# A channel-mix weight split on one Trainium2 core: the sign carried by the slope of a leaky rectifier instead of a join of sign and low bits on VectorE

## Chip, cores and metric

The kernel runs on one core of a Trainium2 chip. The metric is the device time of one execution in microseconds (us); smaller is better. A core has a matrix engine (TensorE, PE in the profile), VectorE (DVE), ScalarE (ACT), GpSimd (POOL) and SyncE (SP), which issues all of this kernel's data transfers. Each engine runs its own instructions strictly in the order in which they were written.

## What is computed

```python
def reference(q, k, v, mem_k, mem_v, moe_mu_k, moe_mu_r, moe_w_k, moe_w_v, moe_w_r):
    # chunked local attention: B=4, H=8, S=768, D=64; 32 queries see 16 + 32 + 8 keys and 8 memory keys
    for c in range(24):
        scores = 0.125 * q_c @ k_full.T
        a = softmax(scores)
        out[:, :, c_start:c_end] = a @ v_full
    x = out.transpose(0, 2, 1, 3).reshape(4, 768, 512)
    # channel mix
    x_prev = x shifted by one token
    xk = mu_k * x + (1.0 - mu_k) * x_prev
    xr = mu_r * x + (1.0 - mu_r) * x_prev
    k = np.maximum(xk @ w_k, 0.0)          # w_k: 512 x 1024
    v = k * k @ w_v                        # w_v: 1024 x 512
    return sigmoid(xr @ w_r) * v           # w_r: 512 x 512
```

The three weight matrices are float64 in memory: they are a normal draw divided by a numpy square root. The other inputs are float32.

## The kernel before

**The products.** The channel mix is done in pairs of float32r numbers: each float32 operand is split into a high part (a cast to float32r) and a low part (the operand minus its high part), and each product is three matmuls, high by high, high by low and low by high.

**The weights.** A weight is loaded as 64-bit words, 1 MB (128 x 1024 words) at a time, in ten chunks: two of `w_r` (raw0, raw1), four of `w_k` (raw2 to raw5), four of `w_v` (raw6 to raw9). For each chunk `weight(i)` makes float32 out of float64 by handling bits:
- `f_abs` (ACT): the upper 32-bit word of each float64, read as a float32, has the sign, 8 of the 11 exponent bits as its exponent, and 3 exponent bits and 20 fraction bits as its fraction. Its absolute value times 2^-112 (`TINY`) moves the exponent so that it fits after a shift. The result goes to `mag`.
- `f_low` (DVE): two instructions, in place in the lower words: the lower word shifted right by 29 (its 3 top bits stay), and then the sign bit of the upper word joined to them.
- `f_join` (DVE): `mag` shifted left by 3, joined with what `f_low` left. That is the float32 weight.
- `f_hi` (ACT or DVE) casts it to float32r, `f_lo` (DVE or POOL) subtracts. The results are `wrh`/`wrl`, `wkh`/`wkl`, `wvh`/`wvl`, which stay in place for the whole kernel.

**The attention** is done in 24 tiles of 128 queries: load `qk` and `vw`, scores `s` (PE), maximum and difference (DVE), exponent (ACT), sum and reciprocal (DVE), the scaling of `e` (DVE or POOL), transposes into `pt` (PE), two copies into `aTz` (ACT or DVE), the product `px` (PE), a copy into `xT` (ACT or DVE).

**The channel mix** is done in 12 units of 256 tokens (two attention tiles): `prep` makes `df`, `xf` and their splits `xh`, `xl` on DVE, ACT and POOL; then PE runs the gate product `pr` (48 matmuls), the first layer `ph` (four blocks of 24 matmuls), and the second layer `pv` (48 matmuls, each of its two token groups in two halves). Between the layers ACT does the rectifier, the square and the cast `kh`, and DVE or POOL `kl`.

**The order.** Nothing is left to a scheduler at run time. A planner in the kernel (`Plan`) holds a list of steps, each with the engine or engines that may do it, a cost in us by the planner's own reckoning, the steps that it needs, and the buffers that it takes. It places the steps one by one on the engine that would finish each first, and the instructions are then written in the order of the planned starts. A changed cost thus moves steps in the order, and from one engine to another. On PE the order of the products is given by a written list (`te_order`). Before the first `ph` block, where the plan leaves PE without work, the loop at the end of the kernel writes fill matmuls on a tile of zeros (`warm`, line 590), one for each 0.22 us of the planned gap. PE runs these in line with its other instructions.

**Buffers.** The loads of `raw` and `qk` share three buffers (`big`): a load waits until the last reader of the load three places earlier has finished. For a weight chunk that last reader is `f_join`. A load of `qk4` waits in this way for the join of raw3, one of raw5 for the join of raw2. `mag`, `df` and `xf` share five (`x4`).

Of the kernel before, what the change touches and what calls it, by code (L numbers as in the profile page):

```python
# [8 lines left out]
F32 = mybir.dt.float32  # L9
F32R = mybir.dt.float32r  # L10
I64 = mybir.dt.int64
U32 = mybir.dt.uint32
AF = mybir.ActivationFunctionType
ALU = mybir.AluOpType
# [14 lines left out]
TINY = 2.0**-112  # L29
# [34 lines left out]
class Plan:  # L64
# [7 lines left out]
    def op(self, alts, fn, deps=(), new=(), use=(), due=1e9):  # L72
        if isinstance(alts, tuple):
            alts = [alts]
        o = Op([(a + (False,))[:3] for a in alts], fn, deps, new, use, due)
        o.seq = len(self.ops)
        self.ops.append(o)
        return o
# [80 lines left out]
def local_attention__then__channel_mix(  # L159
# [11 lines left out]
    nc = tc.nc  # L171
# [10 lines left out]
    def sb(tag, shape, name, dt=F32):  # L182
        return work.tile(shape, dt, tag=tag, name=name, bufs=bufs.get(tag, 1))
# [26 lines left out]
    op = plan.op  # L210
    T = {}

    def copy(e, dst, src):
        if e is nc.scalar:
            e.copy(dst, src)  # L215
        else:
            e.tensor_copy(dst, src)  # L217

    def either(**alts):
        return [(n, *alts[n]) for n in alts]  # L220
# [13 lines left out]
    def weight(i):  # L234
        src, (hi, lo), k = chunks[i]
        h, l = hi[k], lo[k]

        def f_load():
            T["raw", i] = sb("big", [P, 2 * DM], f"raw{i}", I64)
            if src is w_k:  # L240
                nc.sync.dma_start(T["raw", i], src[k * P : (k + 1) * P])
            else:
                nc.sync.dma_start(
                    T["raw", i].rearrange("p (t n) -> p t n", t=2),
                    src[2 * k * P : 2 * (k + 1) * P].rearrange("(t p) n -> p t n", p=P),
                )

        def word(j, dt):
            return T["raw", i].bitcast(dt).rearrange("p (n t) -> p n t", t=2)[:, :, j]

        def f_abs():
            m = T["mag", i] = sb("x4", [P, 2 * DM], f"mag{i}")
            nc.scalar.activation(m, word(1, F32), AF.Abs, scale=TINY)

        def f_low():
            nc.vector.tensor_scalar(word(0, U32), word(0, U32), 29, None, ALU.logical_shift_right)  # L258
            nc.vector.scalar_tensor_tensor(  # L259
                word(0, U32), word(1, U32), 0x80000000, word(0, U32), ALU.bitwise_and, ALU.bitwise_or  # L260
            )

        def f_join():
            mi = T["mag", i].bitcast(U32)
            nc.vector.scalar_tensor_tensor(mi, mi, 3, word(0, U32), ALU.logical_shift_left, ALU.bitwise_or)  # L265

        def f_hi(e):
            copy(e, h, T["mag", i])

        def f_lo(e):  # L270
            e.tensor_sub(l, T["mag", i], h.bitcast(F32))  # L271

        raw, mag = Slot("big"), Slot("x4")
        a = op(("dma", 3.0), f_load, new=[raw])
        b = op(("act", 0.95), f_abs, [a], new=[mag], use=[raw])
        g = op(("dve", 1.75, True), f_low, [a], use=[raw])
        j = op(("dve", 1.15, True), f_join, [b, g], use=[raw, mag])
        hh = op(either(act=(0.95,), dve=(0.62, True)), f_hi, [j], use=[mag])
        ll = op(either(dve=(1.15, True), pool=(2.5, True)), f_lo, [hh], use=[mag])
        wdone[id(hi), k] = (hh, ll)  # L280
# [292 lines left out]
    for i in range(len(chunks)):  # L573
        weight(i)
# [69 lines left out]
```

## Time and profile before

| | us |
|---|---|
| median of 3 runs (lowest to highest) | 447.37 (446.78 to 447.56) |
| the profiled execution, its own time | 446.63 |
| its span, first to last instruction | 444.5 |
| PE busy | 438.9 |
| VectorE busy | 267.2 |
| ScalarE busy | 197.2 |
| GpSimd busy | 30.0 |

The profile's times count from the span's start. Its matmul records overlap (each is listed until its modelled end), so a busy PE is not a PE at its peak, and it is better to compare the starts of successive records. For the other engines too the distance between two starts is a little less than the listed duration when they run back to back. A float32 matmul shows as two records. "Releaser" is the instruction that ended a wait. A line number points into the kernel above; L215 and L217 are the helper `copy`, on ACT and on DVE.

### The profile page before, as it was taken

How to read it: one execution, taken by the hardware profiler on the slowest of the kernel's cores; microseconds unless marked ns; L12 is line 12 of the kernel's file. 1: busy time of each engine (PE TensorE's matmuls, PEld its weight loads, DVE VectorE, ACT ScalarE, POOL GpSimd, SP SyncE). 2: the span in 40 equal slices, each digit the busy share in tenths (PEclk: the TensorE clock that was granted, in tenths of full speed). 3: DMA queues.
4: the chain of work that ended last, by engine and by line, in shares of the span. 5: the costliest groups of instructions: out<-in, count | busy, mean ns of one | idle time of the engine just before them, and what ended most of it. 6: DMA issues, size and time to landing. Idle time of an engine off the chain costs nothing.

```text
span 444.5 us, 8981 instructions
## 1 busy us (share of the span) xinstructions
PE 438.9 (99%) x3946; PEld 390.7 (88%) x3946; DVE 267.2 (60%) x432; ACT 197.2 (44%) x269; POOL 30.0 (7%) x34
## 2 busy tenths in 40 slices
PE   9999999999999999999999999999999999999996
PEld 8899998898898898898898898898898898798894
DVE  3899999986637637636636636636636636612121
ACT  1758398354344345345345345345345345142150
POOL 2100211020010010010010010010010010000000
PEclk9999999999999999999999999999999999999999
DMA  8982928454404404404404404404401200000101
GB/s 329 393 347 98 359 94 316 181 215 143 166 25 144 166 26 142 167 25 143 166 25 143 163 30 143 161 29 143 163 28 47 72 26 1 25 24 1 47 1 47
DMA packets 12902, 55.17 MB, mean 124 GB/s; under 512 B 1472, under 2 KB 1600, under 8 KB 9280
## 3 DMA queue, kind: packets, MB, share of 16 engines
q1 hardware_dynamic: 12864, 54.60, 33.6%
q8 instruction: 31, 0.51, 0.5%
q14 instruction: 7, 0.06, 0.1%
HBM read 48.30 MB, written 6.29 MB: 123 GB/s over the span
## 4 chain that ended last, share of the span: by engine, by line
PE 81%; DVE 14%; issue 2%; ACT 2%; POOL 0%; POOLq 0%; DVEq 0%
PE pv L550 28%; PE ph L494 27%; PE pr L462 13%; PE px L369 5%; PE s L311 4%; DVE mag L265 2%; PE pt L350 2%; DVE raw L259 2%; PE warm L590 2%; DVE raw L258 1%; DVE xf L433 1%; DVE wvl L271 1%; DVE wkl L271 1%; DVE df L433 1%; ACT aTz L215 1%
## 5 line engine op out<-in xcount | busy, mean ns | idle before, releaser
L494 PE MATMUL ph<-xh,wkh 128*128 128x256 f32 x384 | 109.8, 286 | 0.0
L494 PE MATMUL ph<-xh,wkl 128*128 128x256 f32 x384 | 107.8, 281 | 0.0
L494 PE MATMUL ph<-xl,wkh 128*128 128x256 f32 x384 | 107.7, 281 | 0.0
L550 PE MATMUL pv<-wvh,kh 128*128 128x512 f32 x192 | 77.6, 404 | 0.0
L550 PE MATMUL pv<-wvh,kl 128*128 128x512 f32 x192 | 76.1, 396 | 0.0
L550 PE MATMUL pv<-wvl,kh 128*128 128x512 f32 x192 | 75.6, 394 | 0.0
L494 PEld LDWEIGHTS ph<-xh,wkh 128*128 128x128 f32 x384 | 72.3, 188 | 1.2
L519 DVE TENSOR_TENSOR kl<-kf,kh 128x512 fp32r<-128x512 f32 x45 | 32.2, 716 | 68.1 <-ACT kh L215 68.0
L494 PEld LDWEIGHTS ph<-xl,wkh 128*128 128x128 f32 x384 | 72.4, 189 | 0.5
L494 PEld LDWEIGHTS ph<-xh,wkl 128*128 128x128 f32 x384 | 72.4, 188 | 0.0
L502 ACT ACTIVATE kf<-ph 128x512 f32<-128x512 f32 x48 | 28.7, 598 | 85.2 <-PE ph L494 82.6
L550 PEld LDWEIGHTS pv<-wvh,kl 128*128 128x128 f32 x192 | 36.0, 188 | 8.7
L550 PEld LDWEIGHTS pv<-wvh,kh 128*128 128x128 f32 x192 | 36.1, 188 | 8.2
L550 PEld LDWEIGHTS pv<-wvl,kh 128*128 128x128 f32 x192 | 36.1, 188 | 8.0
L590 PE MATMUL warm<-zero_sb 128*128 128x128 f32 x298 | 37.4, 284 | 1.1 <-DVE zero_sb L204 1.1
L462 PE MATMUL pr<-wrh,xl 128*128 128x512 f32 x96 | 38.2, 398 | 0.0
L462 PE MATMUL pr<-wrh,xh 128*128 128x512 f32 x96 | 37.8, 394 | 0.0
L462 PE MATMUL pr<-wrl,xh 128*128 128x512 f32 x96 | 37.8, 393 | 0.0
L590 PEld LDWEIGHTS warm<-zero_sb 128*128 128x128 f32 x298 | 35.6, 198 | 1.6 <-DVE zero_sb L204 1.1
L344 POOL TENSOR_TENSOR e<-e,sum 128x512 f32<-128x512 f32 x11 | 18.5, 1680 | 260.7 <-DVE sum L340 260.7
L217 DVE COPY aTz<-pt 64x512 f32<-64x512 f32 x29 | 20.0, 690 | 25.1 <-PE pt L350 24.9
L425 DVE TENSOR_TENSOR df<-xT 128x1024 f32<-128x1024 f32 x12 | 14.7, 1222 | 28.7 <-ACT xT L215 28.7
(55 smaller groups left out, 577.6 us busy)
## 6 DMA issues: line engine op xcount, KB each, us to landing
qk<-in_qk_dram SPq DMA_DIRECT2D x24, 1024.0 KB, 7.4
vw<-in_vw_dram SPq DMA_DIRECT2D x24, 512.0 KB, 3.7
out_dram<-o SPq DMA_DIRECT2D x24, 256.0 KB, 2.1
raw<-in_w_k_dram SPq DMA_DIRECT2D x4, 1024.0 KB, 5.4
raw<-in_w_v_dram SPq DMA_DIRECT2D x4, 1024.0 KB, 8.0
raw<-in_w_r_dram SPq DMA_DIRECT2D x2, 1024.0 KB, 10.3
id_sb<-in_ident_dram SPq DMA_DIRECT2D x1, 64.0 KB, 8.6
mu_sb<-in_mu_dram SPq DMA_DIRECT2D x1, 4.0 KB, 9.8
```

Of the source, the lines that this page charges most:

```text
L217: e.tensor_copy(dst, src)
L259: nc.vector.scalar_tensor_tensor(word(0, U32), word(1, U32), 0x80000000, word(0, U32), ALU.bitwise_and, ALU.bitwise_or)
L311: nc.tensor.matmul(s4[o : o + 64, j // 2, r, :], q4[:, r, j, :], k4[:, r, j, :], start=True, stop=True)
L344: g.tensor_mul(e, e, T["sum", t].unsqueeze(2).to_broadcast([P, 2 * NPAIR, NK]))
L369: nc.tensor.matmul(p3[64 * h : 64 * h + 64, 2 * g : 2 * g + 2, CHUNK * j : CHUNK * j + CHUNK], v[:, g, h, j, :], a[:, m, g, cc, h, :], sta ...
L425: e.tensor_sub(d, x[:, :, 1:], x[:, :, :UTOK])
L462: nc.tensor.matmul(p, x[:, k, c * P : (c + 1) * P], w, start=(k + n == 0), stop=(k == KT - 1 and n == 2))
L494: nc.tensor.matmul(p[:, i * UTOK : (i + 1) * UTOK], w[:, fc], x[:, k], start=(k + n == 0), stop=(k == KT - 1 and n == 2),)
L502: e.activation(r, T["ph", u, f], AF.Relu)
L519: e.tensor_sub(l, T["kf", u, f], T["kh", u, f].bitcast(F32))
L550: nc.tensor.matmul(p, x[:, tc_], w, start=(f + n == 0), stop=(f == FT - 1 and n == 2))
L590: nc.tensor.matmul(warm[:, :P], zero_sb, zero_sb, start=True, stop=True)
```

## The change

In `f_abs` the function is now a leaky rectifier (`Prelu`) with slope -(2^32) for negative inputs, under the same scale 2^-112. A positive upper word gives what the absolute value gave. A negative one gives the absolute value times 2^32, so that its exponent field is larger by 32; the shift by 3 in `f_join` puts that one bit into the place of the sign. The second instruction of `f_low` is gone, and the planner's cost of `f_low` goes from 1.75 to 0.62.

```diff
         def f_abs():
             m = T["mag", i] = sb("x4", [P, 2 * DM], f"mag{i}")
-            nc.scalar.activation(m, word(1, F32), AF.Abs, scale=TINY)
+            nc.scalar.activation(m, word(1, F32), AF.Prelu, scale=TINY, alpha=-(2.0**32))

         def f_low():
             nc.vector.tensor_scalar(word(0, U32), word(0, U32), 29, None, ALU.logical_shift_right)
-            nc.vector.scalar_tensor_tensor(
-                word(0, U32), word(1, U32), 0x80000000, word(0, U32), ALU.bitwise_and, ALU.bitwise_or
-            )
...
-        g = op(("dve", 1.75, True), f_low, [a], use=[raw])
+        g = op(("dve", 0.62, True), f_low, [a], use=[raw])
```

Because the cost feeds the planner, the order changes from the first weight chunk until about the second unit of the channel mix; behind that PE's order is the same as before. Lines of the changed kernel are one lower than before from `f_join` on (the fills are line 589).

First PE, from the end of the first gate product to the first `ph` block; `warm` are the fills, and the number at a row's end is their count. Before:

```order
L462 MATMUL pr0_406<-wrh1_83,xl0_1_384 128x512
L590 MATMUL warm_100<-zero_sb_88 128x128 x10
L350 MATMUL pt3_469<-id_sb_64,e3_425 128x128 x4
L590 MATMUL warm_100<-zero_sb_88 128x128 x7
L369 MATMUL px3_486<-aTz1_87,vw3_423 64x2x32 x16
L590 MATMUL warm_100<-zero_sb_88 128x128 x33
L311 MATMUL s4_557<-qk4_512 64x64 x16
L590 MATMUL warm_100<-zero_sb_88 128x128 x23
L494 MATMUL ph0_0_619<-xh0_0_477,wkh0_66 128x256
```

And in the changed kernel:

```order
L461 MATMUL pr0_394<-wrh1_83,xl0_1_374 128x512
L349 MATMUL pt3_446<-id_sb_64,e3_410 128x128 x4
L589 MATMUL warm_100<-zero_sb_88 128x128 x15
L368 MATMUL px3_476<-aTz1_87,vw3_435 64x2x32 x16
L589 MATMUL warm_100<-zero_sb_88 128x128 x17
L310 MATMUL s4_527<-qk4_493 64x64 x16
L589 MATMUL warm_100<-zero_sb_88 128x128 x10
L493 MATMUL ph0_0_561<-xh0_0_437,wkh0_66 128x256
```

The products keep their order and number, and the fills between them fall from 73 to 42. Ahead of the gate product they fall from 16 to 8, as these rows show, before:

```order
L369 MATMUL px2_356<-aTz0_86,vw2_303 64x2x32 x16
L590 MATMUL warm_100<-zero_sb_88 128x128 x16
L462 MATMUL pr0_406<-wrh0_82,xh0_1_379 128x512
```

and now:

```order
L368 MATMUL px2_357<-aTz0_86,vw2_303 64x2x32 x16
L589 MATMUL warm_100<-zero_sb_88 128x128 x8
L461 MATMUL pr0_394<-wrh0_82,xh0_1_313 128x512
```

In all 39 fills fewer stand ahead of the first `ph` block.

Next VectorE, up to the last low part that the first `ph` block needs (`wkl3`). Before:

```order
L265 SCALAR_TENSOR_TENSOR mag4_444<-mag4_444,raw4_386 128x1024
L271 TENSOR_TENSOR wkl0_70<-mag2_382,wkh0_66 128x1024
L271 TENSOR_TENSOR wkl1_71<-mag3_421,wkh1_67 128x1024
L271 TENSOR_TENSOR wkl2_72<-mag4_444,wkh2_68 128x1024
L258 TENSOR_SCALAR raw5_504<-raw5_504 128x1024
L259 SCALAR_TENSOR_TENSOR raw5_504<-raw5_504 128x1024
L443 TENSOR_TENSOR xl0_0_522<-df0_305,xh0_0_477 128x1024
L425 TENSOR_TENSOR df1_574<-xT1_376 128x1024
L265 SCALAR_TENSOR_TENSOR mag5_516<-mag5_516,raw5_504 128x1024
L322 TENSOR_REDUCE mx4_579<-s4_557 128x8
L433 SCALAR_TENSOR_TENSOR xf1_584<-df1_574,mu_sb_65,xT1_376 128x256 x4
L271 TENSOR_TENSOR wkl3_73<-mag5_516,wkh3_69 128x1024
```

And in the changed kernel:

```order
L264 SCALAR_TENSOR_TENSOR mag3_429<-mag3_429,raw3_376 128x1024
L217 COPY aTz1_87<-pt3_446 64x16x32
L217 CAST wkh0_66<-mag2_384 128x1024
L442 TENSOR_TENSOR xl0_0_459<-df0_297,xh0_0_437 128x1024
L270 TENSOR_TENSOR wkl0_70<-mag2_384,wkh0_66 128x1024
L260 TENSOR_SCALAR raw5_452<-raw5_452 128x1024
L264 SCALAR_TENSOR_TENSOR mag4_496<-mag4_496,raw4_408 128x1024
L264 SCALAR_TENSOR_TENSOR mag5_500<-mag5_500,raw5_452 128x1024
L270 TENSOR_TENSOR wkl1_71<-mag3_429,wkh1_67 128x1024
L270 TENSOR_TENSOR wkl2_72<-mag4_496,wkh2_68 128x1024
L270 TENSOR_TENSOR wkl3_73<-mag5_500,wkh3_69 128x1024
L321 TENSOR_REDUCE mx4_549<-s4_527 128x8
```

The second instruction of `f_low` is gone. A copy into `aTz` and the cast `wkh0` have come over from ACT (one more `aTz` copy does so earlier, behind the first `f_low`), and `df1`, `mx4` and `xf1` now stand behind `wkl3`. Farther on the casts `xh1_1` and `xh1_0` and the copy `xT2` come over from ACT, and the two `aTz` copies of `pt5` and the cast `wvh3` go to ACT. POOL takes `kl0_0` from VectorE and gives it `kl0_3` and the scaling of `e6`.

Last SP's queue of transfers, from the last chunk of `w_k` on. Before:

```order
L241 DMA raw5_504<-in_w_k_dram 128x1024
L295 DMA qk4_512<-in_qk_dram 128x2048
L295 DMA qk5_520<-in_qk_dram 128x2048
L299 DMA vw5_576<-in_vw_dram 128x1024
L243 DMA raw6_582<-in_w_v_dram 128x2x512
L243 DMA raw7_592<-in_w_v_dram 128x2x512
L299 DMA vw6_768<-in_vw_dram 128x1024
L243 DMA raw8_802<-in_w_v_dram 128x2x512
L243 DMA raw9_835<-in_w_v_dram 128x2x512
```

And in the changed kernel:

```order
L241 DMA raw5_452<-in_w_k_dram 128x1024
L294 DMA qk4_493<-in_qk_dram 128x2048
L298 DMA vw5_503<-in_vw_dram 128x1024
L294 DMA qk5_507<-in_qk_dram 128x2048
L243 DMA raw6_547<-in_w_v_dram 128x2x512
L243 DMA raw7_590<-in_w_v_dram 128x2x512
L243 DMA raw8_725<-in_w_v_dram 128x2x512
L243 DMA raw9_756<-in_w_v_dram 128x2x512
```

Here `vw5` goes ahead of `qk5`, and `vw6` falls behind the last two chunks of `w_v`. Both programs load 22 activation tables on ACT.

## The prediction

> **What bounds the kernel now.** I read the page's busy lines first, then its slices, then the busy time by stage, then the instructions in order of time on PE and VectorE. The page alone misleads:
>
> ```profile
> PE 438.9 (99%) x3946; PEld 390.7 (88%) x3946; DVE 267.2 (60%) x432; ACT 197.2 (44%) x269; POOL 30.0 (7%) x34
> ...
> PE   9999999999999999999999999999999999999996
> ...
> DVE  3899999986637637636636636636636636612121
> ...
> PEclk9999999999999999999999999999999999999999
> ```
>
> PE is busy 99% of the span at full clock, and an edit on VectorE ought to be worth nothing. But VectorE's digits are 9 in the first fifth and 6 or 3 behind it, so there are two stages. Their busy times (columns: stretch, its length, PE, weight loads, VectorE, ACT, POOL, clock, DMA):
>
> ```profile
> 17.30:55.40 38.10, 37.99 (x419) 35.79 (x417) 37.72 (x49) 23.24 (x27) 4.13 (x2) 1.00 0.75 282
> 55.40:95.20 39.80, 39.59 (x355) 35.26 (x354) 38.89 (x54) 26.76 (x36) 6.03 (x5) 1.00 0.58 219
> 95.20:440.70 345.50, 345.44 (x2968) 304.83 (x2968) 182.03 (x314) 141.40 (x200) 15.46 (x16) 1.00 0.24 85
> ```
>
> From 55.4 on PE has 385.03 us of work in 385.30 us. Up to 55.4 VectorE is full (37.72 of 38.10), and much of what PE does is fill (first time is the start, the second the duration; two records to a fill):
>
> ```profile
> 26.89 3.84 PE L590 MATMUL warm<-zero_sb 128*128 128x128 f32 x32
> 30.49 0.48 PE L462 MATMUL pr<-wrh,xh 128*128 128x512 f32 x1
> ...
> 36.17 2.39 PE L590 MATMUL warm<-zero_sb 128*128 128x128 f32 x20
> 38.40 0.60 PE L350 MATMUL pt<-id_sb,e 128*128 128x128 f32 x4
> 38.84 1.73 PE L590 MATMUL warm<-zero_sb 128*128 128x128 f32 x14
> 40.49 1.15 PE L369 MATMUL px<-aTz,vw 128*64 128x64 f32 x32
> 41.58 7.63 PE L590 MATMUL warm<-zero_sb 128*128 128x128 f32 x66
> 49.14 1.15 PE L311 MATMUL s<-qk 128*64 128x64 f32 x32
> 50.22 5.40 PE L590 MATMUL warm<-zero_sb 128*128 128x128 f32 x46
> 55.38 0.36 PE L494 MATMUL ph<-xh,wkh 128*128 128x256 f32 x1
> ...
> 56.77 0.28 PE L494 MATMUL ph<-xh,wkl 128*128 128x256 f32 x1
> ```
>
> So the time is the start of the first `ph` block, 55.38, plus a stretch in which PE never rests. That start is what can move. Neither kernel has any real product between `px2` and `ph` that the other lacks: a gate, `pt3`, `px3`, `s4`.
>
> **The change, part by part.**
>
> *What it takes from VectorE.* These rows show the pair of `f_low` once, the end of the weight work ahead of `ph`, and a cast and a copy of the sizes that move:
>
> ```profile
> 31.04 1.23 DVE L259 SCALAR_TENSOR_TENSOR raw<-raw 128x1024 uint32<-128x1024 uint32 x1
> 32.18 0.68 DVE L326 TENSOR_TENSOR e<-s,mx 128x512 f32<-128x512 f32 x1
> 32.78 0.69 DVE L258 TENSOR_SCALAR raw<-raw 128x1024 uint32<-128x1024 uint32 x1
> ...
> 49.55 1.22 DVE L425 TENSOR_TENSOR df<-xT 128x1024 f32<-128x1024 f32 x1
> 50.68 1.22 DVE L265 SCALAR_TENSOR_TENSOR mag<-mag,raw 128x1024 uint32<-128x1024 uint32 x1
> 51.82 0.68 DVE L322 TENSOR_REDUCE mx<-s 128x8 f32<-128x512 f32 x1
> 52.42 1.66 DVE L433 SCALAR_TENSOR_TENSOR xf<-df,mu_sb,xT 128x256 f32<-128x256 f32 x4
> 54.00 1.21 DVE L271 TENSOR_TENSOR wkl<-mag,wkh 128x1024 fp32r<-128x1024 f32 x1
> ...
> 83.85 0.69 DVE L217 CAST wvh<-mag 128x1024 fp32r<-128x1024 f32 x1
> 84.46 2.35 DVE L271 TENSOR_TENSOR wvl<-mag,wvh 128x1024 fp32r<-128x1024 f32 x2
> ```
>
> The removed instruction takes 1.14 from its start to the next (31.04 to 32.18). Six of the ten stand ahead of `wkl3`: 6.84 us. Added ahead of it are two copies into `aTz` (0.69 each by the group below) and the cast `wkh0` (83.85 to 84.46, 0.61): 1.99. Moved behind it are `df1` (49.55 to 50.68, 1.13), `mx4` (0.60) and `xf1` (1.58): 3.31. `wkl3` ended at 55.21 and now ends at 55.21 - 6.84 + 1.99 - 3.31 = 47.05. Behind it VectorE loses the other four removed instructions.
>
> ```profile
> L217 DVE COPY aTz<-pt 64x512 f32<-64x512 f32 x29 | 20.0, 690 | 25.1 <-PE pt L350 24.9
> ```
>
> *What PE does with it.* PE runs its fills whether they are needed or not, so its start can't come earlier than they allow. The five stretches of fill above, taken from start to start, are 3.60 + 2.23 + 1.65 + 7.56 + 5.16 = 20.20 us for 89 fills, 0.227 each. The 39 that go are worth 8.85 us: the first `ph` block can start at 55.38 - 8.85 = 46.53. It needs `wkl3` at its twelfth matmul, 56.77 - 55.38 = 1.39 later, at 47.92. VectorE gives it at 47.05, 0.87 ahead. So the fills set the start, and VectorE just keeps up.
>
> *The transfers.* This is where the new order is tight. `qk4` may be loaded once raw3 is joined. Counting back in the new VectorE order from `wkl3`: `aTz` 0.69, `wkh0` 0.61, one shift 0.61, and seven instructions of 1.14 (`xl0_0`, `wkl0`, two joins, `wkl1` to `wkl3`) make 9.89, so that join ends at 37.16. `s4` is due on PE at 46.53 - 10 x 0.227 - 1.08 = 43.18. That leaves `qk4` 6.0 us. The rows for such loads (the last: shortest, median, longest time to landing of a `qk`):
>
> ```profile
> 41.02 0.33 SPq L241 DMA_DIRECT2D raw<-in_w_k_dram  x1
> 42.15 1.43 SPq L295 DMA_DIRECT2D qk<-in_qk_dram  x2
> ...
> 46.34 1.20 ACT L255 ACTIVATE mag<-raw 128x1024 f32<-128x1024 f32 x1 [1.62 <-DMA raw<-in_w_k_dram]
> ...
> DMA to landing us min/median/max: 4.8/7.4/11.6
> ```
>
> Bounds: 4.8 costs nothing, 7.4 holds `s4`, and with it all PE behind it, by 1.4. raw5 goes out 1.75 us ahead of it (one join and one shift earlier), where it had 1.13 before, so the two collide less than they did; I take 0.4. raw5 itself took 5.32 from issue to first use (41.02 to 46.34); issued at 35.4 it lands at 40.7, when VectorE comes to its shift (40.74). `vw5` ahead of `qk5`, and `vw6` behind the last weights, cost nothing: their products come more than 10 us later on PE. If DMA were slower, `s5` would be late next.
>
> *Prelu for Abs.* No row shows a Prelu. The nearest is the Abs of the same shape and strides, the first row here:
>
> ```profile
> L255 ACT ACTIVATE mag<-raw 128x1024 f32<-128x1024 f32 x10 | 11.6, 1174 | 2.0 <-DMA raw<-in_w_k_dram 1.6 <-DMA raw<-in_w_v_dram 0.3
> L480 ACT ACT_TABLE_LOAD x11 | 14.1, 1283 | 0.2
> ```
>
> I cost it at 1.17, no difference. Bounds: a shorter one by 0.13 (the plain casts of ACT's kind of row are near 1.04) gains nothing, since the fills set the start; one twice as long puts 1.17 more ahead of each join, at the worst 6 x 1.17 - 0.87 = 6.2 us. What covers a longer one is ACT's idle time, 38.10 - 23.24 = 14.9 us ahead of `ph`, and ACT also loses the copies and casts that VectorE takes over. I take the equal price because only the function differs.
>
> *Behind 46.5.* A tight place is the second half of `pv0_0`, which needs `wvl3`. Durations from the chain that ended last (24 or 12 matmuls, or one `px` or `s`), and the row at which that unit's `pv` began:
>
> ```profile
> 95.81 2.85 PE ph L494 x24
> ...
> 98.66 1.08 PE px L369 x32
> 99.74 0.93 PE s L311 x32
> ...
> 109.76 2.80 PE pv L550 x12
> ```
>
> ```profile
> 75.78 0.48 PE L550 MATMUL pv<-wvh,kh 128*128 128x512 f32 x1
> ```
>
> In the new order the first half of `pv0_0` starts at 75.78 - 8.85 = 66.93 and `px5` ends at 70.81; then come `s6`, half of `pv0_1`, `ph1_0` and `s7`, 7.51 us, and the second half at 78.32 wants `wvl3` at its eighth matmul, 1.63 later: 79.95. VectorE has from `px5` on: `xT2` 0.69, `xl1_0` 1.14, a small fill and `mx6` 0.70, `df2` 1.13, the last join 1.14, a difference 0.60, `xf2` 1.58, `wvl3` 1.21, together 8.19, done at 79.00. It keeps up by 0.95, so I cost this at nothing. On POOL `kl0_0` takes the place of `kl0_3`, and the scaling of e6 comes to VectorE: the first has 20 us until `pv0_0` (66.93 - 46.53), the second stands behind `wvl3`, so neither costs anything. From the second unit on PE's order is the one of before, and the shift reaches the end undiminished.
>
> *Sum.* -8.85 + 0.4 = -8.45. Against the profiled execution's own 446.63 that is 438.18. The median of the runs shown is 0.74 above that execution, so I predict 438.9.
>
> **Rivals.**
>
> *Transfers or VectorE come late.* The margins are 0.87, 0.95 and none for `qk4` at its median. If `qk4` takes 7.4 (1.0 more than I took), and raw8 and raw9 hold VectorE past its 0.95 by another 1 to 2 us, 1 to 3 us come back: 440 to 442. For it: at 17 to 55 VectorE has 0.38 us of slack in all. Against: DMA's share there is 0.75, below full.
>
> *Nothing moves.* If PE's 99% were all work, 447.4. For it: the page. Against it: the fills are in line on PE and 39 of them are gone from the program; it would take a wait of 8.85 us in their place, more than any load of `qk` but the longest.
>
> *Slower: a slow Prelu.* If the slope made ACT take several passes, its place is the join of each chunk. With t more for each of six, all of it ahead of `ph`, 6t - 0.87 is lost; from t = 1.6 (a Prelu of 2.8 us) the gain is gone, and at three times Abs, t = 2.34, the time is 438.9 + 13.2 = 452. Nothing in the trace speaks for it but that there is no row.
>
> *Tables.* If neither the table set of the exponent nor that of the sigmoid held Prelu, ACT would load a set ahead of each group of Prelus: in the new order 8 loads more, four of them ahead of `ph`, at 1.28 each (the row above). That is 5.1 us on ACT, within its 14.9 idle but next to the joins: 438.9 to 444.0. Against it, the changed program has 22 loads as before. On this the Trainium skill, page "ScalarE: Activation LUTs", section "Table sets: the hidden batching unit", speaks against the change: it lists relu, copy, identity and abs as the functions in every set, and Prelu isn't among them. The same page, section "What ACT_TABLE_LOAD costs", puts a switch at 2.66 us with its drain, which would make those eight an estimated 21 us on ACT; the trace's load of 1283 ns agrees with its figure for the load alone.
>
> **How the numbers follow.** The forecast, 437.8 to 440, has 0.63. Late transfers or VectorE, 440 to 443, 0.21. Below 437.8, 0.05: there is little to win under the fills' floor, 446.63 - 8.85 + 0.74 = 438.5, except a few tenths of the profile's own waits and the runs' spread of 0.8. Tables 0.02, within the late range. Nothing moves 0.04. Slow Prelu 0.05. The range 437.7 to 441.6 takes the forecast, nearly all that is below it, and most of the late case: 0.80. Faster by over 0.2% (0.9 us, about what runs of this kernel can tell from no change) 0.91, the same 0.04, slower 0.05.
>
> **What the profile after would show.** If I am right: the `warm` group at x220 records (298 less 78); the first `ph` at 46.5 to 47.5; no `raw<-raw` SCALAR_TENSOR_TENSOR rows; `mag<-raw` on ACT near 1.17; 11 and 11 table loads; the last stage in the same length, its start some 8.5 earlier. I would be wrong if `s4` waits for `qk` by over a microsecond, if PE rests between the first `ph` and the second unit, or if `mag<-raw` is longer than 2 us.

## The result, and the profile after

The changed kernel takes 439.23 us (median of four runs, 439.04 to 440.29), the kernel before in the same comparison 447.47 (446.78 to 448.04). The ratio is 0.9824, 95% interval 0.9811 to 0.9836. That is 8.2 us less by the medians and 7.9 by the ratio, where 8.5 were forecast (438.9, range 437.7 to 441.6). The profiled execution took 439.10 (span 437.3), 7.53 less than the profiled one of before (446.63, span 444.5), which was a little faster than the median of its kernel.

The stages of the changed kernel, cut at its own first `ph` block and at the end of its last wait (columns as before: stretch, length, PE, weight loads, VectorE, ACT, POOL, clock, DMA):

```profile
17.30:47.00 29.70, 29.59 (x343) 27.30 (x342) 29.36 (x40) 21.39 (x24) 0.19 (x1) 1.00 0.86 321
47.00:92.30 45.30, 44.27 (x415) 39.76 (x413) 42.98 (x67) 27.78 (x39) 6.32 (x5) 1.00 0.67 249
92.30:433.50 341.20, 341.09 (x2908) 300.60 (x2908) 177.27 (x303) 139.58 (x198) 15.49 (x16) 1.00 0.23 82
```

VectorE is still full up to the first `ph` (29.36 of 29.70), the last stretch is still PE's alone, and the middle one has something new: PE rests in it for a microsecond. PE from the fills behind `px2` to the first `ph`:

```profile
27.25 2.05 PE L589 MATMUL warm<-zero_sb 128*128 128x128 f32 x16
...
35.17 3.51 PE L589 MATMUL warm<-zero_sb 128*128 128x128 f32 x30
38.62 1.15 PE L368 MATMUL px<-aTz,vw 128*64 128x64 f32 x32
39.70 4.06 PE L589 MATMUL warm<-zero_sb 128*128 128x128 f32 x34
43.69 1.15 PE L310 MATMUL s<-qk 128*64 128x64 f32 x32
44.77 2.50 PE L589 MATMUL warm<-zero_sb 128*128 128x128 f32 x20
47.02 0.36 PE L493 MATMUL ph<-xh,wkh 128*128 128x256 f32 x1
```

Each row starts where the fills ahead of it end: PE is paced by its fills all the way, as before. From 27.25 to 47.02 are 19.77 us, against 28.49 from 26.89 to 55.38 before: 8.72 less, and the 39 fills at 0.227 are 8.85. VectorE gives `wkl3` at 46.8 and the twelfth matmul wants it at 48.4. The rows of VectorE and of the load of `qk4`:

```profile
43.33 3.48 DVE L270 TENSOR_TENSOR wkl<-mag,wkh 128x1024 fp32r<-128x1024 f32 x3
...
37.09 0.33 SPq L294 DMA_DIRECT2D qk<-in_qk_dram  x1
```

The Prelu costs what the Abs cost (1164 ns against 1174), and the table loads are the same:

```profile
L257 ACT ACTIVATE mag<-raw 128x1024 f32<-128x1024 f32 x10 | 11.6, 1164 | 1.0 <-DMA raw<-in_w_v_dram 1.0
L333 ACT ACT_TABLE_LOAD x11 | 14.1, 1283 | 0.9 <-PEq L631 0.7
L479 ACT ACT_TABLE_LOAD x11 | 14.1, 1283 | 0.2
```

What was not forecast is the rest of PE at `px6`. The chain that ended last, with times and durations, shows why:

```profile
83.53 1.70 DVE e L343
85.23 0.60 DVE mx L321
85.83 0.60 DVE o L563
86.43 0.60 DVE e L325
87.03 1.58 DVE df L432 x4
88.61 0.60 DVE o L563
89.21 0.60 DVE sum L337
...
90.28 0.69 DVE e L343
...
91.01 0.70 DVE aTz L217
...
91.73 0.59 ACT aTz L215
...
92.36 1.15 PE px L368 x32
```

`pt6` was ready on PE at 88.2, but its copy on VectorE stands behind the whole softmax of tile 7, `e7` (with two output products `o` and a token mix `df` between its steps), and ACT's half of the copy waits for VectorE's. The first row here is the scaling of `e6`, which came over from POOL. In the kernel before, `s7` stood on PE behind `px6` (starts 99.57 and 98.59), so nothing of tile 7 could come between; in the new order `s7` starts at 78.19, long ahead of `px6`. The last `ph` matmul ahead of `px6` starts at 90.99, so `px6` could have come at about 91.1. It comes at 92.36.

One more thing has to be taken out before executions are compared closely. The first `s` block started at 5.58 in the profile of before, 5.92 in this one, and as late as 6.72 in another (run e7 of the table below; the runs e1 to e7 are not the tiles `e1` to `e7`), whose programs up to there are the same. All that follows is later by that much. The load that `s` reads is not what makes it so late: in all nine profiles it lands 4.7 to 5.1 us behind its issue at 0.74, by 5.9 at the latest, and only in the profile of before does the trace show PE's weight load waiting for it (0.21). It is the 13 fills ahead of it, here before and in run e7:

```profile
1.05 4.50 PE L590 MATMUL warm<-zero_sb 128*128 128x128 f32 x26 [1.05 <-DVE zero_sb L204]
...
1.05 5.74 PE L593 MATMUL warm<-zero_sb 128*128 128x128 f32 x26 [1.05 <-DVE zero_sb L205]
```

Their 26 records start 0.21 us apart at first and 0.11 apart later, and the step changes at 3.9 us in the profile of before, at 4.8 in the changed kernel's, and in run e7's not before their end at 6.5. So this table goes by stretches of the profiled executions, from the start of the fills behind `px2` to the first `ph` and on to the start of the last `o`:

| kernel | fills to `ph` | `ph` to last `o` | together | median of its runs |
|---|---|---|---|---|
| before | 28.49 | 385.29 | 413.78 | 447.47 |
| changed | 19.77 | 386.47 | 406.24 | 439.23 |
| e1: changed work, old order | 28.48 | 384.70 | 413.18 | 446.76 |
| e2: old work and order, fewer fills | 27.04 | 386.74 | 413.78 | 447.26 |
| e3: changed, copies of `pt6` on ACT | 19.78 | 385.27 | 405.05 | 437.93 |
| e4: changed, no `kl` on POOL | 19.78 | 385.37 | 405.15 | 438.35 |
| e5: both of these | 20.17 | 385.37 | 405.54 | 438.61 |
| e6: changed, 7 fills fewer | 18.79 | 387.65 | 406.44 | 439.42 |
| e7: both, 7 fills fewer | 18.49 | 385.27 | 403.76 | 437.41 |

The medians come from three comparisons, in which the kernel before took 447.47 (the first two rows), 447.30 (e1 to e4) and 447.04 (e5 to e7). The ratios below are each to the one of its own comparison.

### The profile page after: what moved, and what is told of

Its sections match the earlier page's. It is cut to its first block, busy times and chain, and to the rows that moved or that the text cites. A ratio compares the mean times of both kernels' runs of the same rounds, so it can differ in the third digit from the quotient of the medians.

```text
span 437.3 us, 8807 instructions
## 1 busy us (share of the span) xinstructions
PE 430.8 (99%) x3868; PEld 382.6 (88%) x3868; DVE 257.8 (59%) x426; ACT 194.2 (44%) x266; POOL 26.4 (6%) x33
## 4 chain that ended last, share of the span: by engine, by line
PE 94%; DVE 3%; ACT 2%; issue 0%
PE ph L493 30%; PE pv L549 30%; PE pr L461 15%; PE px L368 6%; PE warm L589 6%; PE s L310 5%; PE pt L349 2%; ACT aTz L215 1%; DVE e L343 1%; DVE o L563 0%; DVE df L432 0%; DVE mx L321 0%; ACT L333 0%; DVE xl L442 0%; DVE mag L264 0%; DVE df L424 0%
## 5 line engine op out<-in xcount | busy, mean ns | idle before, releaser
L518 DVE TENSOR_TENSOR kl<-kf,kh 128x512 fp32r<-128x512 f32 x45 | 31.1, 691 | 69.7 <-ACT kh L215 69.6
L501 ACT ACTIVATE kf<-ph 128x512 f32<-128x512 f32 x48 | 28.7, 598 | 80.5 <-PE ph L493 80.5
L343 POOL TENSOR_TENSOR e<-e,sum 128x512 f32<-128x512 f32 x10 | 16.7, 1667 | 261.0 <-DVE sum L339 261.0
L333 ACT ACTIVATE e<-e 128x512 f32<-128x512 f32 x24 | 15.2, 632 | 36.3 <-DVE e L325 36.2
L508 ACT ACTIVATE kf<-kf 128x512 f32<-128x512 f32 x48 | 30.3, 631 | 1.2
```

The source lines that it names most:

```text
L333: nc.scalar.activation(e, e, AF.Exp, scale=SCALE)
L343: g.tensor_mul(e, e, T["sum", t].unsqueeze(2).to_broadcast([P, 2 * NPAIR, NK]))
L501: e.activation(r, T["ph", u, f], AF.Relu)
L508: e.activation(q, q, AF.Square)
L518: e.tensor_sub(l, T["kf", u, f], T["kh", u, f].bitcast(F32))
```

## Experiments

**The work without the order, and the fills without the work.** The theory is that the gain needs two things at once, VectorE's shorter work and the fills that the planner drops because of it. Two kernels do one each. The first is the changed kernel with the old cost, which gives back the old order with all 89 fills:

```diff
-        g = op(("dve", 0.62, True), f_low, [a], use=[raw])
+        g = op(("dve", 1.75, True), f_low, [a], use=[raw])
```

> The changed arithmetic (Prelu, no second instruction in f_low) in the order of the kernel before: the planner's cost of f_low is put back to 1.75, so all five engines keep the old order and PE its 89 fills ahead of the first ph block; only VectorE's ten joins of sign and low bits are gone. Theory (the fills set the start of ph, and behind it PE never rests): VectorE is earlier and waits, the first ph starts at 55.4 as before, and the time is that of before, 447.4 within 0.9. Rival (VectorE's work sets the start, the order is secondary): ph starts up to 6.8 us earlier, 440.5 to 442.

Measured: 446.76, ratio 0.9985 (0.9976 to 0.9993). PE's row of the last fills and the first `ph`, the busy times up to 55.4, and what VectorE waited for most in 17 to 56 us:

```profile
51.18 5.40 PE L589 MATMUL warm<-zero_sb 128*128 128x128 f32 x46
56.34 0.36 PE L493 MATMUL ph<-xh,wkh 128*128 128x256 f32 x1
...
17.30:55.40 38.10, 37.98 (x417) 35.74 (x417) 32.24 (x46) 24.38 (x29) 1.51 (x2) 1.00 0.76 284
...
DVE wkl L270 <- ACT wkh L215: 2.6, 1, 2.6
```

VectorE's busy time falls from 37.72 to 32.24 and it now waits for ACT, while PE runs the same fills in the same 28.48 us. The whole of VectorE's relief, 11.4 us by the trace, is worth 0.7 us of 447 when the order stays: the second stretch is 0.59 shorter, 0.21 of it by the small rests of PE between 55 and 95 that are gone (39.80 busy of 39.80 there, 39.59 before). The theory holds. VectorE uses up much of its relief in waits of 6.4 us in this stretch, most of them for ACT, which in turn waited 1.7 for `pr` and 1.6 for `pt3` on PE; so `wkl3` ends at 54.7, 3.0 ahead of its use, where it was 1.6 ahead before.

The second is the kernel before, with 39 fills fewer and nothing else:

```diff
+CUT = {16: 8, 10: 0, 33: 20, 23: 15}
...
                 n = 0 if ("ph", 0, 0) in T else int((o.start - busy - 0.2) / (0.22 if busy else 0.43))
+                n = CUT.get(n, n)
```

> The kernel before, its arithmetic and its order, with 39 fills fewer ahead of the first ph block (16 to 8, 10 to 0, 33 to 20, 23 to 15). Theory (VectorE's 6.84 us had to go as well): PE waits where the fills stood. wkl3 still ends at 55.2 and is wanted by the twelfth matmul, 1.39 behind the start, so the start can't be earlier than 53.8: at most 1.6 us of the 8.85 come, 445.8 to 447.4. Rival (the fills alone were the bound): 8.85 us come, 438.6.

Measured: 447.26, ratio 1.0004 (0.9992 to 1.0015). PE waits where the fills stood:

```profile
38.48 1.05 PE L351 MATMUL pt<-id_sb,e 128*128 128x128 f32 x4 [3.03 <-DVE e L345]
39.33 3.01 PE L592 MATMUL warm<-zero_sb 128*128 128x128 f32 x14
...
49.68 1.15 PE L312 MATMUL s<-qk 128*64 128x64 f32 x32 [1.60 <-DMA qk<-in_qk_dram]
...
54.13 0.36 PE L495 MATMUL ph<-xh,wkh 128*128 128x256 f32 x1
...
17.30:55.40 38.10, 32.92 (x353) 29.91 (x351) 37.72 (x49) 23.29 (x27) 3.79 (x2) 0.96 0.75 282
55.40:95.20 39.80, 38.41 (x344) 34.05 (x342) 38.89 (x55) 26.82 (x35) 6.20 (x4) 1.00 0.55 219
```

`pt3` waits 3.03 for VectorE's scaling and `s4` 1.60 for `qk4`, whose buffer VectorE's join frees. The first `ph` comes 1.45 us sooner, as forecast at most, and all of it is lost again in the stage behind, where PE now rests for 1.39 us (39.80 less 38.41) instead of 0.21: 0.98 and 0.41 at the transposes at 61.06 and 75.61, both for VectorE's scaling of `e`. So before the change the fills and VectorE's work were nearly equally long, twice over: up to the first `ph`, and up to about 76 us. Either alone is worth next to nothing; together, in the new order, they were worth 7.9.

The rows show one thing more. Behind the rest of 3.03 us PE runs at half speed: 14 records of fill take 2.93 us from start to start (39.33 to 42.26), where they took 1.65 before, and the granted clock is 0.51 from 38.7 to 42.1, which makes the 0.96 of the first stretch. All twelve runs of this kernel show a mean clock of 0.992 to 0.996, those of the others 0.998 or more. That cost PE 1.7 us, which the wait for `qk4` covers: VectorE shows no wait in 17 to 56 us, so it isn't held by PE, and it is VectorE's join that lets `qk4` be loaded. So the result stands, but the run shows what the fills keep up, the clock, and that a gap left in their place can cost more than its own length.

Not shown is how much of the 7.9 needs the new order itself (a cast and copies from ACT to VectorE, and `df1`, `mx4` and `xf1` behind `wkl3`): no run has the shorter work and the fewer fills in the old order.

**The rest at `px6`.** Two causes offered themselves, the place of the copy in VectorE's order and a hindrance by POOL. First the copy, with VectorE's half moved to ACT:

```diff
+            go.name = (t, s)
             return go
...
+            if getattr(o.fn, "name", None) in ((6, 0), (6, 1)):
+                o.eng = "act"
```

> The changed kernel with one move: VectorE's half of the copy of pt6 into aTz0 is done by ACT, beside ACT's own half, in the same place of ACT's order. In the changed kernel px6 starts 1.25 us after PE has ended the block ahead of it, because this copy stands on VectorE behind e7's whole softmax (it starts at 91.01, though pt6 is done at 88.2). Theory (that place on VectorE is the whole of the rest): the copies are done by about 90, the wait goes, and the time falls by 1.2 us below the changed kernel's 439.2, to 438.0. Rival (VectorE's backlog shows elsewhere at once, in xT3 or kl1_1): no change within 0.4, 438.8 to 439.6.

Measured: 437.93 (437.79 to 438.49), ratio to the kernel before 0.9790 (0.9777 to 0.9803). Both halves now run on ACT as soon as its rectifier is done, and PE doesn't rest:

```profile
88.64 0.60 ACT L502 ACTIVATE kf<-ph 128x512 f32<-128x512 f32 x1 [0.32 <-PE ph L494]
89.27 1.17 ACT L215 COPY aTz<-pt 64x512 f32<-64x512 f32 x2
```

From `ph` to the last `o` it takes 385.27 us, 1.20 less than the changed kernel, as the theory had it. POOL's hindrance is still there in this run, so it doesn't make the rest alone.

Then POOL. The rows of the changed kernel's VectorE and POOL at two places:

```profile
54.95 1.41 DVE L260 TENSOR_SCALAR raw<-raw 128x1024 uint32<-128x1024 uint32 x1 [0.29 <-DMA raw<-in_w_v_dram]
56.28 3.45 DVE L264 SCALAR_TENSOR_TENSOR mag<-mag,raw 128x1024 uint32<-128x1024 uint32 x2
...
83.45 1.78 DVE L343 TENSOR_TENSOR e<-e,sum 128x512 f32<-128x512 f32 x1
...
54.14 1.67 POOL L518 TENSOR_TENSOR kl<-kf,kh 128x512 fp32r<-128x512 f32 x1 [33.45 <-ACT kh L215]
...
56.37 2.28 POOL L518 TENSOR_TENSOR kl<-kf,kh 128x512 fp32r<-128x512 f32 x1
82.92 1.76 POOL L518 TENSOR_TENSOR kl<-kf,kh 128x512 fp32r<-128x512 f32 x1 [24.27 <-ACT kh L215]
```

```diff
             s, kf, kh, kl = Slot("m"), Slot("kf"), Slot(f"kh{f}"), Slot(f"kl{f}")
+            f_lo.kl = True
...
+            if getattr(o.fn, "kl", False):
+                o.eng = "dve"
```

> The changed kernel with the three kl subtractions that POOL does (kl0_0, kl0_1, kl1_0) on VectorE instead, at their planned places. In the changed kernel three stretches of VectorE are stretched just while POOL runs these: 1.41 for a shift of 0.69, 3.45 for two joins of 2.34, 1.78 for a scaling of 0.69, 2.9 us in all. Theory (the two engines hinder each other, and this is what made VectorE late at px6): VectorE loses 2.9 and gains 1.8 of work, is 1.1 earlier, and the wait of 1.25 at px6 nearly goes: 438.1. Rival (the order alone made it late): VectorE has 1.8 us more to do, the wait grows to 3, 441.

Measured: 438.35 (437.66 to 438.74), ratio 0.9795 (0.9783 to 0.9808). The same VectorE instructions without POOL beside them:

```profile
53.64 1.28 DVE L260 TENSOR_SCALAR raw<-raw 128x1024 uint32<-128x1024 uint32 x2
54.84 2.35 DVE L264 SCALAR_TENSOR_TENSOR mag<-mag,raw 128x1024 uint32<-128x1024 uint32 x2
...
82.49 0.69 DVE L343 TENSOR_TENSOR e<-e,sum 128x512 f32<-128x512 f32 x1
...
89.55 0.69 DVE L217 COPY aTz<-pt 64x512 f32<-64x512 f32 x1
```

Two shifts take 1.28 together, the joins 2.35, the scaling 0.69: the 2.9 us are gone, for 1.8 of added work, and the copy starts at 89.55 instead of 91.01 (0.34 of that is the earlier start of this execution, 5.58 against 5.92). The wait at `px6` is gone too (385.37 from `ph` on). Three subtractions on POOL cost VectorE more than doing them itself. Here the copy stands where it stood, so its place isn't the whole of the rest either, as the theory of the run before had it: both causes were needed, and taking away one is enough. The Trainium skill, page "SBUF — State Buffer", section "Who interferes with whom", says that VectorE and GpSimd share a port pair that one of them holds for a whole instruction, and that a VectorE instruction with two inputs in SBUF contends with a GpSimd one that reads it; the joins (3.45 beside POOL, 2.35 without) agree. The shift, which has one input, was slowed too (1.41 beside POOL, 0.69 without). Whether the pair is held for the whole instruction these runs don't show.

**Both mends, and the fills again.** Three kernels ask whether the two causes add up, and what bounds the time once they are gone.

Both mends together are:

```diff
+            if getattr(o.fn, "name", None) in ((6, 0), (6, 1)):
+                o.eng = "act"
+            if getattr(o.fn, "kl", False):
+                o.eng = "dve"
```

> The changed kernel with both mends: both halves of the copy of pt6 on ACT, and no kl on POOL. Either alone took the wait at px6 away. Theory (that wait of 1.25 us was the only rest of PE behind the first ph block, and the fills set the start): nothing more to win, 438.0 within 0.4, as with either alone. Rival (two separate losses that add up): 436.8.

Measured: 438.61 (437.73 to 438.83), ratio 0.9799 (0.9778 to 0.9821). The median lies 0.2 above the 437.6 to 438.4 of the expectation, and far from the rival's 436.8. By the table this execution lost 0.39 ahead of `ph` (20.17 against 19.78), where `s4` waited 0.33 for `qk4`, and from `ph` on it takes what e4 takes. PE's rest was one wait with two sufficient cures; the second cure adds nothing. In this stretch PE never rests:

```profile
45.00:95.00 50.00, 50.00 (x500) 45.42 (x497) 45.49 (x74) 32.74 (x45) 0.00 (x0) 1.00 0.67 246
```

Then the last fills cut from 10 to 3, once in the changed kernel and once with both mends:

```diff
+CUT = {10: 3}
...
+                n = CUT.get(n, n)
```

> The changed kernel with the last fills ahead of the first ph block cut from 10 to 3 (1.6 us), nothing else. Theory (VectorE's work is as long as the road to px6, so what ph gains comes back there): the first ph starts 1.4 to 1.6 earlier, the wait at px6 grows from 1.25 to about 2.8, and the time stays at 439.2 within 0.5. Rival (the fills are the only bound): 437.6.

Measured: 439.42, ratio 0.9823 (0.9802 to 0.9844), the changed kernel's own. The first `ph` comes 1.0 us sooner by the table, since `s4` also waited 0.51 for `qk4` in this execution, and PE gives it back at two products:

```profile
44.41 1.15 PE L311 MATMUL s<-qk 128*64 128x64 f32 x32 [0.51 <-DMA qk<-in_qk_dram]
...
46.19 0.36 PE L494 MATMUL ph<-xh,wkh 128*128 128x256 f32 x1
...
70.28 1.15 PE L369 MATMUL px<-aTz,vw 128*64 128x64 f32 x32 [0.66 <-ACT aTz L216]
...
92.72 1.15 PE L369 MATMUL px<-aTz,vw 128*64 128x64 f32 x32 [1.48 <-ACT aTz L216]
```

In the same view the changed kernel's wait at `px6` is 1.10, so the two waits here are 1.04 longer together. The expectation had the whole of it at `px6`; some comes back at `px5` already. The time is as the theory said.

> Both mends and the cut of the last fills from 10 to 3. Theory (with VectorE out of the way the fills are the bound again): the first ph starts 1.4 to 1.6 earlier and at least 1.1 of it reaches the end (wvl3 may hold PE by some 0.5): 436.4 to 436.9. Rival (VectorE still ends later than PE wants): no better than the mends alone, 438.0.

Measured: 437.41 (436.53 to 437.81), ratio 0.9775 (0.9750 to 0.9799), the lowest median of all; its interval lies below the changed kernel's, which begins at 0.9811, and overlaps those of the kernels with one mend or both. By the table the first `ph` comes 1.28 sooner than in the changed kernel and nothing comes back (385.27): 403.76 against 413.78 before. Its median missed the 436.4 to 436.9 of the expectation: in its profiled execution, whose 437.41 is the median, the first `s` block started at 6.72, 1.14 later than in that of before, and `s4` waited 0.21. Whether the other four runs lost their time in the same way isn't on record. Taken by stretches it gains 1.3 on the mends alone (405.05 to 405.15), as expected; by medians, 0.5 to 1.2. The runs don't settle more than that.

## Why the prediction was right, and where it was not

- *PE's 99% is two stages, and the start of `ph` is what moves*: right. From `ph` on, before and after differ by 1.18 us in 385.
- *39 fills at 0.227, 8.85 us*: measured 8.72. e1 and e2 show that this term is a floor that both the fills and VectorE's work have to make room for, not a cause by itself. The prediction had both, 0.87 apart.
- *`wkl3` at 47.05, 0.87 ahead of its use*: it ended at 46.8, 1.6 ahead of its use, in an execution that ran 0.36 late. Right in kind, and a little on the safe side.
- *0.4 for `qk4`*: `s4` didn't wait in the changed kernel's profile. In five more executions of this order up to it (e3 to e7) it waited 0, 0, 0.33, 0.51 and 0.21. The bounds of 0 to 1.4 held; the value belongs between 0 and 0.5.
- *Nothing behind 46.5*: this step failed, by 1.25 us. It checked one place, `wvl3`, and went on to the end from there. `wvl3` did come in time, but at 80.5 against a forecast 79.0, for a use at 80.9 (seven matmuls of 0.233 behind 79.27): of a margin of 0.95 about 0.4 was left. The next thing that PE wanted of VectorE, the copy of `pt6`, stood 15 rows on, behind tile 7's softmax, which the new order had put ahead of it. And the sum took VectorE's durations as they are alone, where three stretches were 2.9 us longer beside POOL. One of the three was the scaling of `e6` (1.78 for 0.69), which the prediction had put at nothing because it stands behind `wvl3`; it stands ahead of the copy. The rest lies in the second unit, so the prediction's own sign of being wrong, a rest of PE between the first `ph` and the second unit, stops just short of it. The slowing beside POOL was to be seen in the trace of before, in a `kl` on VectorE that took 1.77 while POOL ran its own, against 0.68 for the like of it:

```profile
64.76 1.77 DVE L519 TENSOR_TENSOR kl<-kf,kh 128x512 fp32r<-128x512 f32 x1
...
70.34 0.68 DVE L519 TENSOR_TENSOR kl<-kf,kh 128x512 fp32r<-128x512 f32 x1
...
64.45 1.54 POOL L519 TENSOR_TENSOR kl<-kf,kh 128x512 fp32r<-128x512 f32 x1 [17.16 <-ACT kh L215]
```

- *Prelu at the price of Abs, no more tables*: right, 1164 ns and 22 loads. The list of the Trainium skill ("ScalarE: Activation LUTs", "Table sets: the hidden batching unit") that lacks Prelu spoke against it; the trace decides otherwise: Prelu ran behind the exponent's loads and behind the sigmoid's without one load more.
- *The late rival* had the right engine and nearly the right size (1 to 3 us; 1.25 came), but not the place or the cause: neither `qk4` nor raw8 and raw9 held PE up. *Nothing moves*: e2 is the kernel in which it would have held, had the order lost its fills and VectorE kept its work.
- What is left of the difference between the profiled executions: -8.72 (fills) + 1.18 (behind `ph`) + 0.36 (the later start) = -7.18, the difference of the last `o`'s start (433.49 to 440.67). The forecast for it was -8.45, 1.27 more.
- That the median came within 0.4 of the forecast (439.23 against 438.9) is in part luck: the 0.4 set aside for `qk4` wasn't needed and paid a third of the rest at `px6`, and the 0.74 added from the profiled execution to the median was 0.13 in the changed kernel. By the profiled executions alone the forecast is 0.92 off (438.18 against 439.10).

## What to carry to other kernels

When an engine reads 99% busy, look for work that is there only to fill; its share of the early stage is the most that a change can win there if the other engine is relieved as well, and its count in the new program is a price that can be read before a run. Where two engines are equally long up to the same point, taking work from one alone wins nothing (0.7 us of 11.4 here), and so does making room on the other alone (0.0 of 8.9); there a gap of 3 us also halved PE's clock for 3.4 us. After such a gain, follow every wait of the bounding engine on the relieved one until the relieved one first rests, not only the tightest that you know.

## What the runs showed of the hardware that I had not expected

- GpSimd's subtractions slowed VectorE by more than they saved: 2.9 us lost for three of them, against 1.8 for doing them there.
- The first block's start differs by up to 1.14 us between executions (5.58 to 6.72), as much as runs of one kernel spread (1.25 for the changed one). In the late ones the first fills run at half pace for longer (0.21 us a record, up to 6.5 us, instead of 3.9); the load had landed by then. The pace is that of e2's fills at a granted clock of 0.51 (2.93 us for 14 records); for the first microseconds the trace shows no clock of its own.
- After a rest of 3.03 us in e2 the granted clock was 0.51 for 3.4 us. The rests of 0.5 to 1.6 us in e2, e6 and the changed kernel left it at 1.00.
- An ACT activation that reads every second 32-bit word took 1164 to 1174 ns for 1024 elements, a cast of as many contiguous ones 1044. The function and the output type differ too, so the runs don't single out the stride.
